# Filler matmuls without a bank dependency, row-form scores and a gate in four pieces, in a planned attention and convolution kernel

## The chip, the core and the metric

The kernel runs on one core of a Trainium2 chip. The core has five engines with queues of their own: TensorE (PE, with its weight loads as PEld), VectorE (DVE), ScalarE (ACT), GpSimd (POOL) and SyncE (SP). The metric is the device time of one execution in microseconds (us).

## The reference

The reference mixes two branches by a gate: `g * a + (1 - g) * b`, where `x` has 2048 rows of 448 values.

```python
g = sigmoid((x * gate_w).sum(-1, keepdims=True))
q = (x @ wq) as 16 heads of 28;  k = x @ wk;  v = x @ wv      # one k and v for all heads
p = softmax(einsum("bhqd,bkd->bhqk", q, k) * 28 ** -0.5)
a = einsum("bhqk,bkd->bhqd", p, v) @ wo
K = einsum("dn,dnl,dn->dl", C, exp(dt * A * l), dt * B).real   # 448 filters, 2048 long
b = causal convolution of x with K, per column, + x * Dskip
```

## The kernel before, in words

**Attention.** The scores are cut into 1024 tiles of 128 keys by 512 queries. Tile t belongs to group t // 64 (one quarter of the queries and four heads), to key block t % 64 // 4, and to head t % 4. The tiles are worked on in 410 *sets* of three and two in turn. Set s has one score step (`qk`), which writes PSUM banks of psS (five are in use in turn), and one exp on ScalarE (L1412), which reads these banks and writes the ring expT, 15 tiles long. A *value step* (`pv`, L1433) multiplies four tiles of the ring by the values and adds them up in bank 6 (psB). After 16 of them VectorE copies the bank (L1157) and normalizes it (L1169). Exps and sets are counted from 0 here.

A score step has two forms. In *row form* (L1357) each tile uses 29 rows of the array, those of its head, so that tiles of different heads run beside each other. In *full form* (L1380) each tile uses all 128 rows with a masked copy of the queries (qM), and the tiles run one behind the other. The last 24 tiles cover 256 queries by two key blocks each (L1368, L1427).

**Convolution.** VectorE builds tables for 14 chunks of 32 columns (L957 to L1008); TensorE multiplies them (the *table product*, L1031, 64 matmuls a chunk) in two halves; VectorE copies each half (L1043), and GpSimd's queue writes it to DRAM (KP). SyncE's queue loads it back as shifted bands T (the *T load*, four DMAs, 56 loads). TensorE convolves (L1098, 128 matmuls for each of 28 convolutions), VectorE scales the result (L1108), TensorE turns it (L1119), and VectorE adds it to O (L1128). Output products of the first three query quarters (L1137) are folded in by L1148. The last quarter ends the kernel: early halves (L1242, added by L1248), the reciprocal of the sums (L1202, L1209, L1228), the product with it (L1232), the last products (L1270, L1276), the adds (L1290, L1293) and the stores.

**What sets the order.** A planner (`schedule`, L188) takes every operation with an estimated duration, its dependencies and a priority (`pr`, smaller goes first). It places them one by one on the engine queues; the engines then work in that order. Dependencies come from the keys that an operation reads and writes (L133 to L155). On TensorE the planner puts in *general fillers* (L1339, matmuls that add zeros) where it expects a pause and little work before it. Beside them there are *warm fillers* (L1333, also adding zeros to bank 6), one for each of 43 early sets (L1398 to L1400). A warm filler writes key `("b", 6)`, so it depends on the value step before it and every later value step depends on it. `opened` (L279) tells whether an accumulation in bank 6 is under way.

**The gate.** Its sigmoid is spread over partitions by matmuls in `prep_gate`: one (L749) is held back until set 30, and four (L760) are one operation, held back until set 35 (`GATE`, L1396). VectorE copies the result (L766), which the convolution needs in L1108.

Of the kernel before, what the change touches and what calls it, by code (L numbers as in the profile page):

```python
# [12 lines left out]
P = 128  # L13
# [35 lines left out]
ROWS = 400  # L49
NEWQ = 15  # L50
# [45 lines left out]
class Prog:  # L96
# [15 lines left out]
    LAZY = {1.15: 200.0, 1.55: 200.0, 1.58: 200.0, 1.6: 200.0}  # L112
    LATE = 1000.0
    FILL, FWIN, FLOW = 215.0, 4000.0, 0.8

    def __init__(self, nc, es):
        self.nc, self.es = nc, es
# [70 lines left out]
    def schedule(self):  # L188
        ops = self.ops
# [11 lines left out]
        ready = {e: [] for e in ENG}  # L201
        rt = [0.0] * n
# [12 lines left out]
        opened = False  # L215
# [8 lines left out]
        while done < n:  # L224
            best = None
            for e in ENG:
                T = free[e]
                for i in ready[e]:
                    o = ops[i]
                    r = max(rt[i], T)  # L230
                    if o.lock is not None:
                        L = min((x for x in locks if x[0] is None), key=lambda x: x[1], default=None)
                        if L is None:
                            continue
                        r = max(r, L[1] + (300.0 if o.pr >= 2 else 0.0))
                    for k in o.comm or ():
                        if k in comm:
                            r = max(r, ops[comm[k]].end)
                    if e == "pe":
                        j = (npe + o.ni - self.FIRST - 1) // self.BLOCK + 1  # L240
                        if j < len(block):
                            r = max(r, block[j])
                            if o.pr >= 1 and block[-1] > r:
                                left = self.FIRST + (len(block) - 2) * self.BLOCK - npe - o.ni
                                r = max(r, block[-1] - left / self.NEED)
                    if o.slot is not None and o.slot[0] == "T" and self.spaced[0] < r < self.spaced[1]:
                        r = max(r, lastT + self.GAP)
                    key = (r, o.pr, i)
                    if best is None or key < best[0]:
                        best = (key, e, i)  # L250
# [25 lines left out]
                mode = o.mode  # L276
            if e == "pe":
                past.append((r, r + o.ns * o.act))
                opened = o.psb == 1 if o.psb else opened  # L279
            if e == "pool" and o.slot is None:  # L280
                for d in reversed(order[e]):
                    if ops[d].slot is None:
# [148 lines left out]
class Kernel:  # L431
# [311 lines left out]
    def prep_gate(self):  # L743
        pg = self.pg
        X = ("gx",)
        px = self.grp()
        ogT = Sub(self.acc, 512)
        self.gate = []
        o = pg.op("pe", lambda e: e.matmul(px.v(0, 16, 0, [[1, 128]]), self.gt.v(0, P, 16, [[1, 16]]),  # L749
                                       self.identg.v(0, P, 0, [[1, P]]), start=True, stop=True, tile_position=(0, 0),  # L750
                                       skip_group_check=True), 400,
              rd=["og", ("kst", 0)], wr=[X], pr=2, lock=px)
        self.gate.append(o.i)
        pg.op("dve", lambda e: e.tensor_copy(ogT.v(0, 16, 0, [[1, 128]]), px.v(0, 16, 0, [[1, 128]])), 200,
              rd=[X], wr=[("acc", 1)], pr=2)

        def mm(e):
            for mu in range(2):
                for par in range(2):
                    r = e.matmul(px.v(0, P, 64 * mu, [[1, 64]]), self.sel.v(0, 16, 128 * (1 + (1 - mu) - par), [[1, P]]),  # L760
                                 ogT.v(0, 16, 64 * par, [[1, 64]]), start=(par == 0), stop=(par == 1), tile_position=(0, 0),
                                 skip_group_check=True)
            return r
        o = pg.op("pe", mm, 800, rd=[("acc", 1)] + [("sel", k) for k in range(3)], wr=[X, "onw"], pr=2)
        self.gate.append(o.i)
        pg.op("dve", lambda e: e.tensor_copy(self.omq.v(0, P, 0, [[1, 128]]), px.v(0, P, 0, [[1, 128]])), 200,  # L766
              rd=[X], wr=["omq"], pr=2, unlock=px)
# [543 lines left out]
    def main(self):  # L1311
# [32 lines left out]
        def qk(s):  # L1344
            ts = sets[s]
            bs = [bank[t] for t in ts]
            bk = [("b", b) for b in bs]

            def row(e):
                if ts[0] >= NLAST:  # L1350
                    for x in range(2):
                        for t, b in zip(ts, bs):
                            r = part(e, t, b, x, True)
                    return r
                for t, b in zip(ts, bs):
                    i, kt, h = dec(t)
                    r = e.matmul(self.psS.v(0, P, 512 * b, [[1, 512]]),  # L1357
                                 kT.v(32 * h, DH + 1, 128 * kt, [[1, 128]]),
                                 qT.v(32 * h, DH + 1, 512 * (i % 2), [[1, 512]]),
                                 start=True, stop=True, tile_position=(32 * h, 0), skip_group_check=True)  # L1360
                return r

            def part(e, t, b, x, row):
                half, kt, h = declast(t)
                kt += x
                o = self.psS.v(0, P, 512 * b + 256 * x, [[1, 256]])
                if row:
                    return e.matmul(o, kT.v(32 * h, DH + 1, 128 * kt, [[1, 128]]),  # L1368
                                    qT.v(32 * h, DH + 1, 512 + 256 * half, [[1, 256]]),
                                    start=True, stop=True, tile_position=(32 * h, 0), skip_group_check=True)  # L1370
                return e.matmul(o, kT.v(0, P, 128 * kt, [[1, 128]]),
                                self.qM.v(0, P, XQ + 512 * h + 256 * half, [[1, 256]]),
                                start=True, stop=True, tile_position=(0, 0), skip_group_check=True)

            def full(e, t, b):
                if t >= NLAST:
                    part(e, t, b, 0, False)
                    return part(e, t, b, 1, False)
                i, kt, h = dec(t)
                return e.matmul(self.psS.v(0, P, 512 * b, [[1, 512]]), kT.v(0, P, 128 * kt, [[1, 128]]),  # L1380
                                self.qM.v(0, P, (i % 2) * XQ + 512 * h, [[1, 512]]),
                                start=True, stop=True, tile_position=(0, 0), skip_group_check=True)
            if s < 6 or s >= 14 and (len(ts) == 3 or ts[0] % 64 < NEWQ or s >= ROWS):
                rd = set()
                for t in ts:
                    i, kt, h = dec(t)
                    rd |= {("q", i % 2), ("kT", (kt if t < NLAST else declast(t)[1]) // 4)}
                o = pg.op("pe", row, 220, rd=sorted(rd, key=str), wr=bk, pr=0, mode="q", ni=2 * len(ts))
                o.act = 0.25 * len(ts)
            else:  # L1390
                for t, b in zip(ts, bs):
                    i, kt, h = dec(t)
                    kt = kt if t < NLAST else declast(t)[1]
                    o = pg.op("pe", lambda e, t=t, b=b: full(e, t, b), 220, rd=[("qM", i % 2), ("kT", kt // 4)],
                              wr=[("b", b)], pr=0, mode="f", ni=2)
            if s in GATE:  # L1396
                pg.after[self.gate[GATE.index(s)]] = o.i
            if s < WARM and ts[0] % 64 < 52 and (ts[0] < 64 or ts[0] % 64 > 14):  # L1398
                f = pg.op("pe", warm, 215, rd=[("cst", 1), "id"], wr=[("b", 6)], pr=1.95)
                pg.after[f.i] = o.i  # L1400
            if s == len(sets) - 2:
                pg.after[o.i] = self.prevset
            self.prevset = o.i
            if s in STORES:
                self.hold.append(o.i)
            es = [ring[t] for t in ts]
            ew = [("e", x) for x in es]
            for t in ts:
                x = ring[t] if t <= RING else 0
                ew += ["Wk"] if x == RING - 1 else ["Wv", "Wvg", "Wm"] if x == RING - 2 else self.xk(2) if 9 <= x < 13 else self.xk(3) if 5 <= x < 9 else []  # L1410
            n = len(ts)
            o = pg.op("act", lambda e: e.activation(expT.v(0, P, 512 * es[0], spread(es, n)),  # L1412
                                                self.psS.v(0, P, 512 * bs[0], spread(bs, n)),
                                                AF.Exp, scale=SQ), 46 + 428 * n, rd=bk, wr=ew, pr=0)
            self.lastexp = o.i
# [118 lines left out]
```

## Time and profile before

| what | value |
|---|---|
| three runs, median | 501.88, 501.09, 500.85; 501.09 us |
| profiled execution | 500.49 us, span 498.7 us |
| mean granted TensorE clock | 0.999 |
| busy: PE, DVE, ACT, POOL | 478.2, 456.0, 484.6, 197.5 us |
| exps (L1412), 410 | 464.8 us busy, 3.5 us idle before them |
| scores, row form (L1357), 684 | 95.7 us busy |
| scores, full form (L1380), 316 | 95.1 us busy |
| general fillers (L1339), 154 | 49.4 us busy (47.2 on psB, 2.2 on psS) |
| warm fillers (L1333), 43 | 16.1 us busy |

A profiled line of a group gives line, engine, operation, the tile written and the tiles read, shapes, count, then busy time, mean ns of one, and the idle time before them with the instruction that ended it. A line of a timeline gives start in us, duration in us, engine, line, operation and count; in brackets stands an idle time and what ended it. Matmuls of a group overlap, so a busy TensorE is not one at its peak: a matmul of 512 columns takes 0.38 us from start to end, and the next may start 0.22 us behind it. Times from one exp to the next are taken from the start times in the trace.

### The profile page before, as it was taken

What the parts mean: (1) busy time and instruction counts of PE and PEld (TensorE: products, weight loads), DVE (VectorE), ACT (ScalarE), POOL (GpSimd) and SP (SyncE); (2) the same over time, 40 slices, a digit from 0 to 9 for tenths busy, and PEclk for the clock granted to TensorE, in tenths of its full rate; (3) what the DMA queues carried; (4) which work ended last, traced back from release to release, by engine and by line L of the source; (5) the groups of instructions that cost most, each with busy time, mean ns of one, the idle gap of its engine ahead of it and who ended that gap; (6) DMA issues with size and microseconds to landing.
All of it is one profiled execution on the core that took longest, in us unless ns stands there. A gap on an engine that the chain in (4) does not pass through costs nothing.

```text
span 498.7 us, 17357 instructions
## 1 busy us (share of the span) xinstructions
PE 478.2 (96%) x7643; PEld 217.7 (44%) x7643; DVE 456.0 (91%) x868; ACT 484.6 (97%) x436; POOL 197.5 (40%) x362
## 2 busy tenths in 40 slices
PE   8899999999999999999999999999999999999997
PEld 6432242453434435453452543545334354445543
DVE  6999999999999999999999999989999999992225
ACT  6999989999999999999999999999999999999995
POOL 8411034342242466276265456552733342521110
PEclk9999999999999999999999999999999999999999
DMA  8945008719248783945729595594690849657842
GB/s 252 268 57 113 1 16 229 213 34 315 77 118 265 204 217 87 308 108 165 242 36 268 155 288 138 141 220 112 171 265 19 231 129 340 213 164 215 257 131 70
DMA packets 91767, 85.44 MB, mean 171 GB/s; under 512 B 24970, under 2 KB 86716, under 8 KB 91692
## 3 DMA queue, kind: packets, MB, share of 16 engines
q1 hardware_dynamic: 80794, 72.49, 49.8%
q0 software_dynamic: 10624, 11.70, 10.5%
q8 instruction: 60, 0.98, 0.8%
q10 hardware_dynamic: 274, 0.14, 0.1%
q14 instruction: 15, 0.12, 0.1%
HBM read 76.36 MB, written 5.23 MB: 164 GB/s over the span
## 4 chain that ended last, share of the span: by engine, by line
ACT 77%; PE 15%; DMA 2%; SPq 0%; issue 0%
ACT expT L1412 77%; PE psS L1380 2%; PE psS L1357 2%; PE psB L1433 2%; DMA T<-KP_scratch 2%; PE psX L1098 1%; PE psS L1098 1%; PE psS L1031 1%; PE psB L1333 1%; PE psS L1368 1%; PE psS L1242 0%; PE psB L1427 0%; SPq L166 0%; PE psX L1031 0%; PE psX L1119 0%; PE psB L1339 0%
## 5 line engine op out<-in xcount | busy, mean ns | idle before, releaser
L1412 ACT ACTIVATE expT<-psS 128x1536 bf16<-128x1536 f32 (+1 forms) x410 | 464.8, 1363 | 3.5 <-PE psS L1357 1.4
L972 DVE TENSOR_TENSOR tab<-tab,mbf 128x512 bf16<-128x512 bf16 (+4 forms) x140 | 139.2, 996 | 0.0
L1357 PE MATMUL psS<-qT,kT 29*128 29x512 bf16 x684 | 95.7, 385 | 10.5 <-ACT expT L1412 6.4
L1433 PE MATMUL psB<-expT,vaug 128*32 128x512 bf16 x1000 | 99.7, 390 | 0.2 <-DVE acc L1157 0.2
L1380 PE MATMUL psS<-qM,kT 128*128 128x512 bf16 x316 | 95.1, 383 | 0.8
L166 POOL DMA_DIRECT2D KP_scratch<-kstg x104 | 58.1, 565 | 75.5 <-DVE kstg L1043 74.0
L987 DVE TENSOR_TENSOR tab<-tab 128x256 bf16<-128x256 bf16 (+4 forms) x140 | 77.0, 571 | 0.0
L1433 PEld LDWEIGHTS psB<-expT,vaug 128*32 128x32 bf16 x1000 | 25.6, 93 | 72.9 <-issue 69.9
L1357 PEld LDWEIGHTS psS<-qT,kT 29*128 29x128 bf16 x684 | 23.7, 91 | 62.9 <-ACT expT L1412 51.9
L166 POOL DMA_DIRECT2D U<-in_A_x_dram x60 | 39.9, 669 | 25.0 <-DMA U<-in_A_x_dram 10.3
L166 POOL DMA_DIRECT2D qM<-qT x64 | 32.5, 516 | 39.4 <-DVE qT L889 29.3
L1339 PE MATMUL psB<-ident,one 128*128 128x512 bf16 x146 | 47.2, 384 | 0.0
L1098 PEld LDWEIGHTS psS<-T,U 128*26 128x26 bf16 (+3 forms) x1792 | 35.7, 138 | 14.9 <-issue 10.2
L166 POOL DMA_DIRECT2D rdenB<-R_scratch x60 | 31.0, 523 | 28.0 <-DMA R_scratch<-denT 27.9
L1098 PE MATMUL psS<-T,U 128*26 128x128 bf16 (+3 forms) x1792 | 41.0, 226 | 1.1 <-DMA T<-KP_scratch 1.1
L1098 PE MATMUL psX<-T,U 128*26 128x128 bf16 (+3 forms) x1600 | 38.9, 227 | 0.7 <-issue 0.7
L1098 PEld LDWEIGHTS psX<-T,U 128*26 128x26 bf16 (+3 forms) x1600 | 32.6, 139 | 11.9 <-issue 9.5
L166 POOL DMA_DIRECT2D denT<-acc x15 | 10.8, 717 | 56.4 <-DVE acc L1157 47.7
L1001 DVE TENSOR_TENSOR tab<-tab,tmp 128x1984 bf16<-128x1984 bf16 x28 | 32.5, 1177 | 0.0
L1380 PEld LDWEIGHTS psS<-qM,kT 128*128 128x128 bf16 x316 | 19.5, 97 | 24.8 <-ACT expT L1412 15.3
L995 DVE TENSOR_TENSOR tmp<-tmp,mq 128x64 bf16<-128x64 bf16 (+4 forms) x70 | 25.3, 361 | 0.3
L918 DVE TENSOR_TENSOR msq<-T 128x512 f32<-128x512 f32 (+1 forms) x40 | 24.6, 616 | 0.0
(191 smaller groups left out, 511.9 us busy)
## 6 DMA issues: line engine op xcount, KB each, us to landing
T<-KP_scratch SPq DMA_DIRECT2D x212, 272.0 KB, 5.6
rdenB<-R_scratch POOLq DMA_DIRECT2D x60, 64.0 KB, 2.5
U<-KP_scratch SPq DMA_DIRECT2D x12, 272.0 KB, 4.9
U<-in_A_x_dram SPq DMA_DIRECT2D x20, 112.0 KB, 4.6
qM<-qT POOLq DMA_DIRECT2D x64, 32.0 KB, 3.9
tab<-in_A_x_dram SPq DMA_DIRECT2D x4, 448.0 KB, 5.2
KP_scratch<-kstg POOLq DMA_DIRECT2D x104, 16.0 KB, 1.7
xT<-XS_scratch POOLq DMA_DIRECT2D x3, 448.0 KB, 4.3
```

The source lines that it names most:

```text
L166: return [e.dma_start(o, i, **kw) for o, i in pairs]
L918: pg.op("dve", lambda e: e.tensor_tensor(m2(msq), z2, z2, ALU.mult), el(2 * n), rd=[kr, ki] + first, wr=["msq"], pr=pr)
L972: mul = lambda e, o, a, b: e.tensor_tensor(o, a, b, ALU.mult)
L987: vo(lambda e, dv=dv, tv=tv, k=k: e.tensor_tensor(dv, dv, tv, ALU.add if k else ALU.subtract), n, [kt[k], kd[k]], [kd[k]], 1.92 if lv else ...
L995: vo(lambda e, w=w, lv=lv: e.tensor_tensor(rho.v(0, P, (32 - 2 * w) * 2, [[64, 32], [2, w], [1, 2]]), rho.v(0, P, (32 - w) * 2, [[64, 32], ...
L1001: vo(lambda e, k=k: e.tensor_tensor(tab.v(0, P, FM + k * FP + 2, [[64, 32], [2, 31], [1, 2]]), tab.v(0, P, lm + k * PL + 62, [[64, 32], [- ...
L1098: r = e.matmul(ps.v(32 * j, 32 - m0, 128 * k, [[1, 128]]), self.U.v(0, P, (4 * gi + j) % UA // UC * UW + (2 * m0 + par) * UC + (4 * gi + j ...
L1339: return e.matmul(t.v(0, P, off, [[1, 512]]), self.one.v(0, P, 2, [[0, P]]), self.ident.v(0, P, 0, [[0, 4], [1, P]]), start=b != 6, stop=b ...
L1357: r = e.matmul(self.psS.v(0, P, 512 * b, [[1, 512]]), kT.v(32 * h, DH + 1, 128 * kt, [[1, 128]]), qT.v(32 * h, DH + 1, 512 * (i % 2), [[1, ...
L1380: return e.matmul(self.psS.v(0, P, 512 * b, [[1, 512]]), kT.v(0, P, 128 * kt, [[1, 128]]), self.qM.v(0, P, (i % 2) * XQ + 512 * h, [[1, 51 ...
L1412: o = pg.op("act", lambda e: e.activation(expT.v(0, P, 512 * es[0], spread(es, n)), self.psS.v(0, P, 512 * bs[0], spread(bs, n)), AF.Exp, ...
L1433: r = e.matmul(self.psB.v(32 * h, 32, 0, [[1, 512]]), vaug.v(0, P, 32 * kt, [[1, 32]]), expT.v(0, P, 512 * ring[t], [[1, 512]]), start=(kt ...
```

## The change

There are three edits, and a rule in the planner that goes with the first.

- A warm filler no longer names bank 6 as written, so it neither waits for value steps nor holds them back. Instead it is marked `psb = 3`. The planner places such an operation only while `opened` holds. If an operation of priority 0 or less becomes ready while the filler would run (up to 40 ns before its end), the filler's start is put behind it. A filler leaves `opened` as it is.
- A set of three tiles is always in row form; before, sets 6, 8, 10 and 12 were in full form.
- The gate's four matmuls are four operations, of which only the first is held back until set 35.

```diff
+    NEAR = 40.0
...
+                    if o.psb == 3:
+                        if not opened:
+                            continue
+                        for x in ready["pe"]:
+                            if ops[x].pr <= 0.0 and r < rt[x] < r + o.ns - self.NEAR:
+                                r = max(rt[x], T) + ops[x].ns
...
-                opened = o.psb == 1 if o.psb else opened
+                opened = o.psb == 1 if o.psb in (1, 2) else opened
...
-        def mm(e):
-            for mu in range(2):
-                for par in range(2):
-                    r = e.matmul(px.v(0, P, 64 * mu, [[1, 64]]), self.sel.v(0, 16, 128 * (1 + (1 - mu) - par), [[1, P]]),
-                                 ogT.v(0, 16, 64 * par, [[1, 64]]), start=(par == 0), stop=(par == 1), tile_position=(0, 0),
-                                 skip_group_check=True)
-            return r
-        o = pg.op("pe", mm, 800, rd=[("acc", 1)] + [("sel", k) for k in range(3)], wr=[X, "onw"], pr=2)
+        for mu in range(2):
+            for par in range(2):
+                o = pg.op("pe", lambda e, mu=mu, par=par: e.matmul(
+                    px.v(0, P, 64 * mu, [[1, 64]]), self.sel.v(0, 16, 128 * (1 + (1 - mu) - par), [[1, P]]),
+                    ogT.v(0, 16, 64 * par, [[1, 64]]), start=(par == 0), stop=(par == 1), tile_position=(0, 0),
+                    skip_group_check=True), 200, rd=[("acc", 1)] + [("sel", k) for k in range(3)], wr=[X, "onw"], pr=2)
+                if mu + par == 0:
+                    o1 = o
+        o = o1
         self.gate.append(o.i)
...
-            if s < 6 or s >= 14 and (len(ts) == 3 or ts[0] % 64 < NEWQ or s >= ROWS):
+            if s < 6 or len(ts) == 3 or s >= 14 and (ts[0] % 64 < NEWQ or s >= ROWS):
...
-                f = pg.op("pe", warm, 215, rd=[("cst", 1), "id"], wr=[("b", 6)], pr=1.95)
+                f = pg.op("pe", warm, 215, rd=[("cst", 1), "id"], pr=1.95)
+                f.psb = 3
```

Since the planner works through all operations anew, the order of TensorE, VectorE, GpSimd and SyncE changes over the whole kernel.

## Prediction

> **What bounds the kernel now.** I read the page first: the chain that ended last, then the groups.
>
> ```profile
> ACT 77%; PE 15%; DMA 2%; SPq 0%; issue 0%
> ...
> L1412 ACT ACTIVATE expT<-psS 128x1536 bf16<-128x1536 f32 (+1 forms) x410 | 464.8, 1363 | 3.5 <-PE psS L1357 1.4
> ```
>
> The chain is ScalarE's 410 exps, one behind the other; 15% of it is TensorE, where an exp waited. So the question is how often the exps wait. I took their start times from the trace. From one exp to the next it is 1.331 us after three tiles and 0.904 us after two (medians). 205 of the one and 204 of the other make 457.3 us, but the first exp starts at 21.71 and the last at 491.82, 470.1 us later. 2.6 of the 12.8 us between are other ScalarE work behind the first exp. So 10.2 us are lost, and a change of TensorE's order can win no more than that ahead of the last exp. The larger losses: 0.65 us together ahead of exps 6, 8, 10, 12 (0.13, 0.27, 0.13, 0.11); 0.53 ahead of exp 36; 1.27 ahead of exp 42; 1.08 ahead of exp 266; 1.83 in six pieces from 460 to 479 us. The other 4.8 us are small pieces.
>
> The timelines of ScalarE, then of TensorE, show three of these places:
>
> ```profile
> 34.01 31.97 ACT L1412 ACTIVATE expT<-psS 128x1536 bf16<-128x1536 f32 x28 [0.16 <-PE psS L1380]
> 66.20 6.88 ACT L1412 ACTIVATE expT<-psS 128x1536 bf16<-128x1536 f32 x6 [0.23 <-PE psS L1357]
> 74.19 5.97 ACT L1412 ACTIVATE expT<-psS 128x1536 bf16<-128x1536 f32 x5 [1.11 <-PE psB L1433]
> ```
>
> ```profile
> 64.85 0.77 PE L760 MATMUL psS<-acc,onT 16*128 16x64 f32 x5
> 65.35 0.39 PE L1357 MATMUL psS<-qT,kT 29*128 29x512 bf16 x2
> 65.46 0.49 PE L760 MATMUL psS<-acc,onT 16*128 16x64 f32 x3
> 65.79 0.38 PE L1357 MATMUL psS<-qT,kT 29*128 29x512 bf16 x1
> ...
> 72.78 0.60 PE L1333 MATMUL psB<-ident,cst 128*128 128x512 bf16 x2
> 73.22 0.59 PE L1380 MATMUL psS<-qM,kT 128*128 128x512 bf16 x2
> 73.74 0.40 PE L1433 MATMUL psB<-expT,vaug 128*32 128x512 bf16 x4
> 74.08 0.39 PE L1333 MATMUL psB<-ident,cst 128*128 128x512 bf16 x1
> 74.40 0.40 PE L1433 MATMUL psB<-expT,vaug 128*32 128x512 bf16 x4
> ...
> 327.50 0.40 PE L1098 MATMUL psS<-T,U 128*32 128x128 bf16 x12 [1.12 <-DMA T<-KP_scratch]
> ```
>
> At 64.85 the gate's matmuls (one operation, eight records) stand ahead of a score set. At 72.78 value matmuls (L1433) come late, two warm fillers (L1333) among them: none ran between 68.36 and 73.74, and the exp waits for a place in the ring of 15 tiles. At 327.50 a convolution waits for its T load, and the scores behind it with it.
>
> **The change, part by part.** The built order of the changed kernel has the same counts but for: 12 more scores in 29-row form and 12 fewer in full form, 6 fewer general fillers (L1339: 151 for 154 with all banks); warm fillers stay at 43. Everything else is a new order, chosen by the planner. Each part is compared set by set.
>
> *Rows (sets 6, 8, 10, 12).* Three full-form scores take 0.81 us (33.16, L1380 x3), three in row form 0.39 (L1357 x3). That is 0.42 per set, more than any of the four losses. TensorE pays three warm fillers behind set 7 (0.22 each), but sets 6 and 7 with these come to about 2.65 us and the pairs beside them to 2.1, against 2.235 of exps. I take -0.55; ends -0.65 and 0.
>
> *Gate.* The four matmuls now stand two behind set 35, one behind 36, one behind 37. Ahead of set 36 there is half of the 0.9 us, but a value step and a filler stand there too. I take -0.35; ends -0.53 and +0.2.
>
> *Fillers without the bank.* Before, each warm filler wrote bank 6, so every later value step depended on it. In the new order, sets 38 to 46 have a value step at nearly every place that is due, between pieces of the table product (L1031), and the three in a row are gone. The ring is then never full. I take -1.2 of the 1.27; ends -1.27 and -0.6. What is late next: set 40 and set 42 behind 16 table matmuls (0.6), some 0.1 us, within that.
>
> *The T wait at 327.* A side effect. This load was issued at 317.12, behind convolution matmuls of set 257, and landed at 327.46. In the new order those stay in set 257, but the first use moves from behind set 265 to behind set 266, 1.13 us later, with a filler ahead of it: just the wait. I take -1.0; ends -1.08 and 0.
>
> *The stretch from 460 to 479.* Here TensorE has as much work as ScalarE. With durations from this stretch (40 conv matmuls 0.74, a value step 0.3, a row set 0.32), sets 380 to 399 hold 22.9 us of it before and 22.0 after, against 22.4 of exps. One 0.69 us wait at 469.0 has no releaser ("issue"), and T loads land one behind the other there; both can come again. I take -0.5; ends -1.5 and +0.8.
>
> *New waits for T loads.* I compared, load by load, landing and first use. The table products come 2 sets later nearly everywhere (0 to 4), the convolutions 0 to 15 sets later, 6 earlier in one place. Two loads lose cover: the 38th had 1.54 us and is used 1 set closer to its issue; the 41st had 2.06 us, its table product is one set later and its use one set earlier, which leaves about -0.2. I take +0.5 for these and other unplanned waits; ends 0 and +1.5.
>
> *DVE as cover.* VectorE idles under 4 us from 20 to 449, and its last table ends at 448.6; the table products started 0.2 to 4.3 us behind their tables. If ScalarE runs 3 us ahead, this would be late next. But those products are 2 sets (2.24 us) later in the order, and VectorE's own 1.16 us wait at 330 goes with the T wait. So I charge nothing; without that cover it would cost up to 1 us.
>
> *The tail.* Behind the last exp (end 492.41) the order is longer. Before:
>
> ```profile
> 493.69 0.21 DVE L1228 RECIPROCAL T<-psS 128x8 f32<-128x8 f32 x1
> 493.90 0.62 DVE L1290 TENSOR_TENSOR O<-O,psS 128x448 bf16<-128x448 bf16 x1
> 494.70 0.42 DVE L1232 TENSOR_TENSOR onT<-acc,psS 128x256 bf16<-128x256 f32 x1 [0.18 <-PE psS L1217]
> 495.58 0.62 DVE L1290 TENSOR_TENSOR O<-O,psS 128x448 bf16<-128x448 bf16 x1 [0.46 <-PE psS L1270]
> ```
>
> One add of 0.62 stands between the reciprocal and the product that the last outputs need (L1232). In the new order two stand there (L1248 and L1290), since the last convolution's transposes (16 of L1119, 0.45 us) and the early outputs of tile 15 moved behind the last exp. Two adds from a reciprocal that ends near 494.16 end at 495.3, so L1232 starts at about 495.24, +0.54. Behind it stand four output matmuls, not two: 0.93 us for 0.55, +0.38. Together +0.9; ends +0.5 and +1.5. The store of columns 320 on (issued 490.05, last packet 492.9) comes after the last exp too, but its packets would end about 4.3 us behind that exp, ahead of the last tiles' packets.
>
> **Sum.** -0.55 -0.35 -1.2 -1.0 -0.5 +0.5 +0.9 = -2.2 us. The profiled execution took 500.49 us (498.7 of span and 1.8 around it), 0.6 under the median of the three runs shown, 501.09. So 498.3 profiled, and 498.9 as a median. This measurement can tell about 0.2% from no change, 1.0 us.
>
> **Rivals.**
>
> *Taken back (0.16).* The transfers and the "issue" waits are drawn anew with any order, and as many come as went: the T wait and the late stretch are then of no worth, new waits 1.0. That gives -0.55 -0.35 -1.2 +1.0 +0.9 = -0.2, 500.9. For it: 4.8 us of small losses that I can't place. Against: only two waits near 1 us in the whole trace came from a load or from "issue".
>
> *More (0.15).* The late stretch keeps pace (-1.5), nothing new waits, tail +0.7: -3.9, 497.2. For it: 22.0 us of work in 22.4.
>
> *Clock (0.06), the slower side.* Ahead of the first value step four warm fillers go (24.21 to 27.04), since the bank isn't open yet. From 24.0 to 27.4 TensorE was busy for 82% of the time; four times 0.22 us less leave 57%. If the granted clock halves for 3.4 us there, half of that work, 1.7 us, comes late, and ScalarE waits for it. One such stretch gives 500.6; two give -2.2 + 3.4, 502.3, and that is slower than before. It decides from 1.3 stretches on. Against it stands the emptiest stretch before, here with the columns TensorE busy, weights, VectorE, ScalarE, GpSimd, granted clock, DMA share, GB/s:
>
> ```profile
> 12.00:14.00 2.00, 0.87 (x12) 0.56 (x10) 2.00 (x3) 1.90 (x2) 1.79 (x4) 1.00 1.06 250
> ```
>
> TensorE is busy for 0.87 of 2 us, and the clock stays at 1.00. The Trainium skill ("TensorE: Matmul & The Clock Gate", section "A second HAM failure mode: psum-queue depth-cycling") says that cycling through PSUM banks with 512-column matmuls leaves short pauses in which the clock falls and rises again. By that rule this kernel would show it before the change already; the trace disagrees, its mean granted clock is 0.999.
>
> *It doesn't do what it says (0.01):* the built order shows that it does.
>
> The forecast itself has 0.62 (497.9 to 499.9). Faster by over 0.2%, under 500.1: 0.62 + 0.15, and 0.03 of the first rival, 0.80. Within 0.2%: 0.13. Slower: 0.07, the clock and the worst of what is taken back. The range leaves about a tenth out on either side: 497.2 to 501.0.
>
> **What would show it.** Right: exps 6 to 12 at 0.904 us behind the one before; no exp behind L1433 near 73; under 0.3 us lost at exp 36; no wait at exp 266, but perhaps at exp 327; L1232 some 2.8 us behind the last exp's end (2.29 before) and the last L1293 some 4.3 (3.36). Wrong: a granted clock under 1.00 between 20 and 40 us; L1031 waiting for DVE tab in the sum; more than 1 us lost at new places between 80 and 450 us.

## The result and the profile after

The changed kernel took 497.74 us (median of 5, 497.46 to 498.08), the kernel before on the same chip 501.01 (median of 5, 500.31 to 501.88): ratio 0.9934, 95% interval [0.992, 0.9949]. On a second chip it took 496.88 beside 500.78, ratio 0.9913 [0.9894, 0.9931]. So it gained 3.3 and 3.9 us where 2.2 were forecast. Its first profiled execution took 498.08 us with a span of 496.3, clock 0.999; the one of before took 500.49 and 498.7.

The page of after, the chain by engine and the group of the exps:

```profile
ACT 86%; PE 8%; issue 0%
...
L1421 ACT ACTIVATE expT<-psS 128x1536 bf16<-128x1536 f32 (+1 forms) x410 | 464.1, 1347 | 1.0 <-PE psS L1388 0.6
```

TensorE's share of the chain is 8% for 15%, and the exps (now L1421; lines from the gate on are 8 or 9 higher) waited 1.0 us for 3.5. The timeline of ScalarE from 28 to 80 us, where before had three waits, is one row without a bracket:

```profile
27.60 53.14 ACT L1421 ACTIVATE expT<-psS 128x1024 bf16<-128x1024 f32 x47
```

The timeline of TensorE shows why. The gate's matmuls, two records each, no longer stand ahead of the score set of exp 36 as one block: two run beside it. From 69 us on a value step (L1442) stands between the pieces of the table product (L1039), with no filler among them; and at 324.85 a convolution finds its T load there:

```profile
63.90 0.32 PE L766 MATMUL psS<-acc,onT 16*128 16x64 f32 x1
64.06 0.38 PE L1365 MATMUL psS<-qT,kT 29*128 29x512 bf16 x1
...
69.16 0.40 PE L1442 MATMUL psB<-expT,vaug 128*32 128x512 bf16 x4
69.49 0.42 PE L1039 MATMUL psX<-tab 128*64 128x128 bf16 x8
69.84 0.60 PE L1388 MATMUL psS<-qM,kT 128*128 128x512 bf16 x2
70.38 0.40 PE L1442 MATMUL psB<-expT,vaug 128*32 128x512 bf16 x4
...
324.85 0.47 PE L1106 MATMUL psX<-T,U 128*32 128x128 bf16 x16
```

The timeline of VectorE behind the last exp, which ended at 488.69:

```profile
490.05 0.21 DVE L1236 RECIPROCAL T<-psS 128x8 f32<-128x8 f32 x1 [0.20 <-PE psS L1210]
490.26 0.62 DVE L1256 TENSOR_TENSOR O<-O,psS 128x448 bf16<-128x448 bf16 x1
490.80 0.61 DVE L1298 TENSOR_TENSOR O<-O,psX 128x448 bf16<-128x448 bf16 x1
491.44 0.42 DVE L1240 TENSOR_TENSOR onT<-acc,psS 128x256 bf16<-128x256 f32 x1
```

Two adds stand between the reciprocal and the product, as forecast. The product starts 2.75 us behind the last exp's end (2.29 before), the last copy (L1301, 492.88) 4.19 (3.36), and the span ends 7.6 behind it (6.34).

The two spans differ by 2.4 us: the exps lose 3.3 less, the tail takes 1.3 more, and the first exp starts 0.44 earlier (21.27 for 21.71). Over all profiles below the first exp starts at 21.27 to 22.28, whatever the kernel, so that part is not the change's.

### The profile page after: what moved, and what is told of

Same layout as the page of the kernel before. It is cut to its first block, busy times and chain, and to the rows that moved or that the text cites. A ratio compares the mean times of both kernels' runs of the same rounds, so it can differ in the third digit from the quotient of the medians.

```text
span 496.3 us, 17350 instructions
## 1 busy us (share of the span) xinstructions
PE 476.6 (96%) x7640; PEld 217.8 (44%) x7640; DVE 455.5 (92%) x868; ACT 483.8 (97%) x436; POOL 196.2 (40%) x362
## 4 chain that ended last, share of the span: by engine, by line
ACT 86%; PE 8%; issue 0%
ACT expT L1421 86%; PE psX L1106 1%; PE psS L1388 1%; PE psB L1442 1%; PE psS L1365 1%; PE psS L1376 1%; PE psS L1106 0%; PE psS L1250 0%; PE psB L1436 0%; PE psS L1278 0%; PE psX L1127 0%; PE psS L1145 0%; PE psB L1347 0%; PE psS L1225 0%; PE psS L1210 0%
## 5 line engine op out<-in xcount | busy, mean ns | idle before, releaser
L1421 ACT ACTIVATE expT<-psS 128x1536 bf16<-128x1536 f32 (+1 forms) x410 | 464.1, 1347 | 1.0 <-PE psS L1388 0.6
L1365 PE MATMUL psS<-qT,kT 29*128 29x512 bf16 x696 | 97.4, 384 | 9.2 <-ACT expT L1421 4.8
L1442 PE MATMUL psB<-expT,vaug 128*32 128x512 bf16 x1000 | 100.3, 390 | 0.5 <-issue 0.5
L1388 PE MATMUL psS<-qM,kT 128*128 128x512 bf16 x304 | 92.0, 384 | 1.4 <-issue 0.7
L1442 PEld LDWEIGHTS psB<-expT,vaug 128*32 128x32 bf16 x1000 | 25.6, 93 | 71.7 <-issue 69.6
L1106 PE MATMUL psX<-T,U 128*26 128x128 bf16 (+3 forms) x1792 | 44.2, 226 | 0.2 <-DVE O L1136 0.2
L1106 PEld LDWEIGHTS psX<-T,U 128*26 128x26 bf16 (+3 forms) x1792 | 37.2, 138 | 14.6 <-issue 10.0
L1106 PE MATMUL psS<-T,U 128*26 128x128 bf16 (+3 forms) x1600 | 37.7, 226 | 0.0
L1106 PEld LDWEIGHTS psS<-T,U 128*26 128x26 bf16 (+3 forms) x1600 | 32.4, 138 | 11.4 <-issue 8.0
L1388 PEld LDWEIGHTS psS<-qM,kT 128*128 128x128 bf16 x304 | 18.5, 97 | 23.5 <-ACT expT L1421 14.5
```

The lines of the kernel that those rows point to most:

```text
L1106: r = e.matmul(ps.v(32 * j, 32 - m0, 128 * k, [[1, 128]]), self.U.v(0, P, (4 * gi + j) % UA // UC * UW + (2 * m0 + par) * UC + (4 * gi + j ...
L1365: r = e.matmul(self.psS.v(0, P, 512 * b, [[1, 512]]), kT.v(32 * h, DH + 1, 128 * kt, [[1, 128]]), qT.v(32 * h, DH + 1, 512 * (i % 2), [[1, ...
L1442: r = e.matmul(self.psB.v(32 * h, 32, 0, [[1, 512]]), vaug.v(0, P, 32 * kt, [[1, 32]]), expT.v(0, P, 512 * ring[t], [[1, 512]]), start=(kt ...
```

## The experiments

Each profile was read in one way: the time from one exp to the next over 1.331 or 0.904 us, summed by stretches of exps. "Under 1" counts the executions with a mean granted clock of 0.997 or less. The ratio is to before on the same chip. "Listed" kernels keep an order that is written out.

| kernel | median, before | ratio, 95% | under 1 | exps 1-13 | 14-34 | 35-50 | 51-260 | 261-280 | 281-380 | 381-409 | sum | behind |
|---|---|---|---|---|---|---|---|---|---|---|---|---|
| before, first profile | 501.01 | | | 1.0 | 0.1 | 1.8 | 2.6 | 1.2 | 1.3 | 2.1 | 10.2 | 6.3 |
| p_rows (listed) | 500.40, 500.65 | 0.9995 [0.9979, 1.0011] | 6 of 12 | 0.3 | 0.5 | 1.9 | 3.8 | 0.3 | 1.4 | 2.4 | 10.6 | 6.3 |
| p_ring (listed) | 500.26, 500.65 | 0.9997 [0.9977, 1.0017] | 6 of 12 | 1.0 | 0.1 | 1.3 | 2.8 | 0.7 | 1.2 | 1.7 | 8.8 | 6.4 |
| p_load (listed) | 500.30, 500.65 | 0.9994 [0.9982, 1.0005] | 4 of 11 | 1.1 | 0.1 | 1.8 | 2.6 | 0.6 | 1.3 | 2.4 | 9.9 | 6.3 |
| p_all (listed) | 500.26, 500.65 | 0.9986 [0.9972, 1.0001] | 5 of 12 | 0.3 | 0.5 | 1.5 | 2.8 | 0.6 | 1.3 | 1.2 | 8.3 | 6.4 |
| p_clk (listed) | 499.42, 500.22 | 0.9979 [0.9965, 0.9993] | 0 of 12 | 1.0 | 0.1 | 1.8 | 2.7 | 0.7 | 1.2 | 2.7 | 10.3 | 6.4 |
| rows | 500.16, 500.78 | 0.9984 [0.9967, 1.0001] | 1 of 12 | 0.3 | 0.2 | 2.0 | 3.0 | 0.6 | 1.3 | 1.6 | 9.0 | 6.9 |
| fill | 501.72, 500.78 | 1.0014 [0.9999, 1.0029] | 11 of 12 | 1.1 | 0.1 | 0.7 | 3.7 | 1.8 | 1.7 | 1.6 | 10.6 | 6.7 |
| no_gate | 500.35, 500.22 | 0.9988 [0.9969, 1.0008] | 6 of 12 | 0.3 | 0.2 | 0.7 | 3.5 | 0.6 | 1.9 | 1.9 | 9.1 | 7.5 |
| no_fill | 499.06, 500.22 | 0.9976 [0.9956, 0.9995] | 6 of 12 | 0.3 | 0.2 | 1.9 | 3.4 | 2.0 | 1.4 | 1.1 | 10.2 | 6.4 |
| after, first profile | 497.74, 501.01 | 0.9934 [0.9920, 0.9949] | 1 of 5 | 0.3 | 0.2 | 0.2 | 3.0 | 0.2 | 2.6 | 0.4 | 6.9 | 7.6 |
| after_2 | 496.88, 500.78 | 0.9913 [0.9894, 0.9931] | 0 of 6 | 0.3 | 0.2 | 0.2 | 3.0 | 0.2 | 1.1 | 1.2 | 6.3 | 7.4 |
| tail (listed) | 497.22, 500.78 | 0.9941 [0.9912, 0.9969] | 4 of 12 | 1.3 | 0.2 | 0.2 | 3.0 | 0.2 | 1.1 | 0.5 | 6.6 | 7.3 |
| tail_f (listed) | 497.40, 500.22 | 0.9945 [0.9924, 0.9965] | 2 of 7 | 0.3 | 0.2 | 0.2 | 3.0 | 0.2 | 1.1 | 0.6 | 5.7 | 7.5 |

The stretches and the time from the end of the last exp to the end of the span (last column) are those of one profile of each kernel, and some losses come and go between executions of one order. Four of these profiles (p_rows, fill, no_fill, tail) hold one fall of the clock each between the first exp and the last. Of the executions of before, 49 of 94 had a clock of 0.997 or less, and took 501.05 for 499.90 (medians).

### One wait at a time, in the old order

The theory after the result: each edit takes its wait away for good. The rival: the luck of a new order, or a later wait that takes it back. So the order of before was written out for all engines, and the planner takes the next operation of the list:

```diff
+            tok = seq.pop(0)
...
                 for i in ready[e]:
+                    if tok >= 0 and i != tok:
+                        continue
                     o = ops[i]
```

**p_rows**: the 29-row edit, its operations in the old places.

```diff
-            if s < 6 or s >= 14 and (len(ts) == 3 or ts[0] % 64 < NEWQ or s >= ROWS):
+            if s < 6 or len(ts) == 3 or s >= 14 and (ts[0] % 64 < NEWQ or s >= ROWS):
```

> The order of before is written out on every engine and kept; only the three score matmuls of sets 6, 8, 10 and 12 become 29-row ones. Theory (each wait that is removed stays removed): exps 6, 8, 10, 12 start 0.90 to 0.91 us behind the one before, 0.65 us less is lost there, the last exp starts 0.6 us earlier and the kernel takes 500.4 for 501.0. Rival 1 (taken back): the exps are ahead by 0.65 at exp 12, but a later wait for a load, a table or a value step gives it back, so the last exp starts as before and the time is 501.0. Rival 2 (the gain of the whole change is the luck of a new order): makes no difference to this kernel, whose order is the old one; then the parts held in the old order must together fall well short of 3 us.

**p_ring**: TensorE's order from set 40 on (s score set, k eight table matmuls, v value step, f warm filler; the text on record counts these sets one too low). The warm fillers of sets 36 to 49 name no bank:

```diff
-s40 k k s41 k k k s42 f f s43 v f v f f v s44 f v
+s40 v k k s41 v k k k s42 f f s43 v f f f s44 v f
```

> The order of before but for four value steps, which stand one to three sets earlier (behind sets 39, 40, 42 and 43), ahead of the warm fillers that held them back; the warm fillers of sets 36 to 49 do not name bank 6, the others do. Theory: the loss ahead of exp 42 falls from 1.27 to under 0.3 us and stays away; 499.8 for 501.0. Rival 1 (taken back): the loss at exp 42 goes, but the table products behind it, or a later wait, take it back within some sets, and the time is 500.8 to 501.0.

**p_load**: 44 convolution matmuls (c, four each) behind set 267.

```diff
-c c c s266 c c c c c c c c s267 v c
+s266 s267 v c c c c c c c c c c c c
```

> The order of before but for the first 11 operations (44 matmuls) of the convolution that waited for its T load at 327: they stand behind set 267 and its value step, two sets later. Theory: no wait at exp 266, the load has landed by the first use; 1.0 us less, 500.0 for 501.0. Rival 1 (taken back): TensorE has no room for the 0.8 us that it skipped, or the next T load, whose buffer comes free later, is waited for: the loss moves to exps 268 to 290 and the time is 500.7 to 501.0.

**p_all**: the three together, and the gate in four operations.

> The three edits of the other kernels of this call in one, and the gate's four matmuls apart (two behind set 35, one behind 36, one behind 37), else the order of before. Theory: 0.65 + 1.27 + 1.08 + 0.35 = 3.3 us less ahead of the last exp and the tail of before kept: 497.7 for 501.0, as much as the changed kernel gained with a longer tail. Rival 1: the later waits take back half or more, over 499.4. Rival 2 (luck of the new order, mainly the stretch from 460 to 479): this kernel still loses its 1.8 us there, and ends at or above 499.

Measured: at its own place each edit did at least part of what it should, but for p_load. Exps 1 to 13 lose 0.3 for 1.0 in p_rows and p_all. Exps 35 to 50 lose 0.5 less in p_ring; 0.58 stays at exp 42, because in the old order three pieces of the table product stand behind the value step that now comes in time:

```profile
71.42 0.61 PE L1470 MATMUL psS<-qM,kT 128*128 128x512 bf16 x2
71.96 0.40 PE L1523 MATMUL psB<-expT,vaug 128*32 128x512 bf16 x4
72.29 0.89 PE L1121 MATMUL psS<-tab 128*64 128x128 bf16 x24
73.12 0.39 PE L1447 MATMUL psS<-qT,kT 29*128 29x512 bf16 x3
```

But the times hardly fell: 0.4 us or less by the medians, and p_all, forecast at 497.7, took 500.26. Both theories lose something. Part is taken back: with 0.7 won at exps 1 to 13, exps 14 to 34 lose 0.4 more, as a value step then waits 0.6 us for VectorE to copy bank 6 (0.60 in p_rows, 0.58 in p_all). And the T wait at 327 had been one execution's: p_rows, p_ring and p_clk keep that part of the old order, and in their profiles no convolution waits there (exps 261 to 280 lose 0.3 to 0.7, not 1.2). Two of them wait for another load instead, at 338, for 0.35 (p_ring) and 0.30 us (p_clk). p_load took away what is mostly not there.

### The edits alone, planned anew

**after_2** is the changed kernel once more. **fill** and **rows** are before with one edit each, the first and the second of the change's diff.

> The changed kernel once more, beside kernels with one edit, since the times of the kernel before spread from 499.1 to 503.2 us on the last chip. If the first measurement holds, 3.3 us under the kernel before of this call (ratio 0.993) and the exps lose some 7 us as in its first profile (first exp to last exp start 466.8 us). If the gain was half the luck of that chip or of its profile, the ratio is 0.996 or more.

> The kernel before with the filler edit alone (no bank in the keys, and the planner's rule), planned anew: table products 0.9 sets later on the mean, 2.1 in the changed kernel. Theory A (the direct waits): exp 42 loses nothing, 0.6 to 1.3 us less; the small waits of exps 6 to 12 and 36 stay; 499.9 for 501.0. Theory B (the new order itself, by later table products and convolutions, is what gains): more than its own wait, 2 us or more less, 499.0 or under.

> The kernel before with the row-form edit alone, planned anew. Theory A: the 0.65 us of exps 6 to 12 go, exps 36 and 42 stay, 0.4 less by the median (what the same edit gave in the old order at full clock), 500.6 for 501.0. Theory B: any new order can gain or lose 1 to 2 us; then it lies more than 1 us away from that, on either side.

The gain of the whole change held, with 3.9 us. The edits alone gave none of it that the intervals tell from nothing: rows 0.6 us less, fill 0.9 us more. In fill the ring wait is gone (exps 35 to 50 lose 0.7, which is the gate), so the edit does its work; but its profile loses 1.0 more than the first of before from 51 to 260 and 0.6 more from 261 to 280, and 11 of 12 executions had a lower clock. The trace places most of that. Of the first, 0.76 is exp 238, where the clock stands at one half from 292.2 on (the two rows below, with the columns TensorE busy, weights, VectorE, ScalarE, GpSimd, granted clock, DMA share, GB/s); of the second, 0.74 is exp 271, behind a wait of TensorE of 1.09 us that nothing in the profile released ("issue").

```profile
288.70:291.70 3.00, 2.01 (x21) 0.55 (x20) 3.00 (x5) 3.00 (x4) 0.75 (x2) 1.00 0.88 231
292.20:295.60 3.40, 3.40 (x31) 1.16 (x27) 3.40 (x4) 2.73 (x3) 0.79 (x2) 0.50 0.97 263
```

**no_gate** and **no_fill** are the changed kernel with one edit undone (no_fill also without the planner's rule that goes with it):

```diff
-        for mu in range(2):
-            for par in range(2):
-                o = pg.op("pe", lambda e, mu=mu, par=par: e.matmul(
+        o = pg.op("pe", mm, 800, rd=[("acc", 1)] + [("sel", k) for k in range(3)], wr=[X, "onw"], pr=2)
```

```diff
-                f = pg.op("pe", warm, 215, rd=[("cst", 1), "id"], pr=1.95)
-                f.psb = 3
+                f = pg.op("pe", warm, 215, rd=[("cst", 1), "id"], wr=[("b", 6)], pr=1.95)
```

> The changed kernel with the gate's matmuls as one operation again, planned anew. Theory A (the edits' own waits): 0.35 us more than the changed kernel, some 3 us under before. Theory B (most of the gain beside 0.7 at exps 1 to 13 and 1.6 at exps 35 to 50 is the draw of a new order: load and instruction waits, late stretch, clock dips): more than 1 us from the changed kernel, most likely slower.

> The changed kernel without the filler edit (29-row sets and the gate in four), planned anew. Theory A: the ring wait of 1.3 us at exp 42 is back, exps 1 to 13 and 36 are as in the changed kernel, 1.0 to 1.2 us under before. Theory B: more than 1 us away from that; by the rows alone (0.16% under before) and the filler edit alone (0.14% over it) anything from 499 to 501.5 where before takes 500.8.

For the whole time this speaks for the order. Without the gate's split, worth 0.4 us at its place, the kernel takes 500.35, as much as before: exps 51 to 260 lose 0.6 more, 281 to 409 1.4 more than in after_2, and half of the executions have a lower clock. In its profile 2.8 us of the loss stand at exps 200, 377 and 397, each behind an "issue" wait (0.92, 0.52 and 1.49 us). Without the filler edit the median is 499.06, which the direct sum had right. Its profiled execution took 500.21; the ring wait is back in it (1.78 at exp 42), and it lost 1.76 at exp 264 for a T load and 0.68 at exp 82, where the clock had fallen at 116.6. Two of these waits in the timelines of TensorE:

```profile
325.75 0.40 PE L1099 MATMUL psS<-T,U 128*32 128x128 bf16 x12 [1.74 <-DMA T<-KP_scratch]
```

```profile
475.31 0.64 PE L1105 MATMUL psS<-T,U 128*32 128x128 bf16 x28 [1.49 <-issue]
```

Such pieces hide what the edits do. Leave out of each sum the pieces of 0.4 us or more that stand behind a T load, a fall of the clock or an "issue" wait: six profiles of the old order keep 7.9 to 8.5 us, rows 8.2, fill 8.1, no_fill 7.8, no_gate 6.3, and four of the changed order (after, after_2, tail, tail_f) 5.6 to 5.8. What is left in no_gate and no_fill is 0.7 and 2.1 more than in the changed order, not far from their own waits (0.4 and 1.7), as theory A has it; the whole time goes with theory B, since a new order also draws these pieces anew. This rests on one profile of each kernel, and rows and fill alone stay in or near the range of the old order.

### The clock

Where the clock fell, the windows show it. The columns are as above. First p_rows, then the kernel called tail below:

```profile
173.00:176.00 3.00, 1.90 (x16) 0.49 (x16) 3.00 (x5) 3.00 (x4) 1.36 (x3) 1.00 0.88 269
176.30:179.70 3.40, 3.40 (x29) 1.11 (x27) 3.08 (x4) 2.35 (x3) 2.23 (x5) 0.51 0.92 293
```

```profile
24.30:27.30 3.00, 1.74 (x24) 0.98 (x21) 3.00 (x8) 3.00 (x5) 0.79 (x1) 1.00 0.93 201
27.60:31.00 3.40, 3.40 (x17) 0.72 (x16) 3.40 (x5) 2.52 (x3) 0.00 (x0) 0.54 0.42 16
```

In both, TensorE was busy for some 0.6 of 3 us, then the clock was one half for 3.4 us, and an exp came late: exp 134 of p_rows by 1.2 us (the text on record below calls it 133), exp 4 of tail by 1.0. The two other falls followed pauses that were less empty: 2.01 of 3 us in fill, and 2.17 of 3 us from 113.3 in no_fill. Other executions pass the same pause at full clock: in the profile of after_2, TensorE is busy for 1.74 of the 3 us from 23.8 and the clock stays at 1.00. The Trainium skill ("TensorE: Matmul & The Clock Gate", section "Part 1: The HAM clock gate (the "warmup" mystery)") says that the gate watches activity in a free-running window of about 3.4 us. That agrees with the 3.4 us measured, and a window that does not start with the kernel would explain why the same order loses the clock in some executions only; no run here shows the window itself.

**p_clk**: the order of before with three fillers in the pause at 173 and one in that at 116.

```diff
-s131 v s132 v s133
+s131 v f f s132 v f s133
```

> The order of before with four more general fillers, three where TensorE was busy for only 0.64 of 3 us (from 172.7, sets 131 and 132) and one at 116 (0.70). In an execution of the same order with 29-row sets the granted clock fell to half from 176.3 on, and 1.2 us were lost at exp 133; of the executions of before, 18 in 35 on one chip and 23 in 29 on the other had a mean granted clock under 1.000, and took 1.3 us longer than the others by the median. Theory (these dips come from the pause at 173, in executions where the clock's window falls on it): nearly all executions at 1.000, and the median falls by 0.7 to 1.2 us, to that of the executions of before at full clock. Rival (the dips fall anywhere or come with the chip): as many dips as in before, no gain.

It held: none of 12 executions under 1, 499.42 for 500.22, with the same losses ahead of the exps as before. Since both pauses were filled, the run does not tell them apart. The places fit in the other kernels too: rows, with TensorE busy for 2.86 of the 3 us from 172.7, had 1 of 12; fill, with pauses at 24, 289 and 330, had 11 of 12.

**tail** and **tail_f** test the longer tail and the pause at 24; tail_f has both of the edits below, tail the first.

```diff
-        for tt in range(4):
+        for tt in range(3):
             self.early(tt)
...
-                for g in range(2, 3):
+                for g in range(2 if tt < 3 else 0, 3):
```

> The changed kernel, its order kept up to the last exp. Behind it the early output of tile 15 is no operation of its own: its two matmuls go into the accumulation of the last output, so that VectorE has one add of 0.62 less between the last reciprocal and the product, and the last value matmul stands directly behind the reciprocal on TensorE. Theory (the longer tail is these adds and matmuls): the product starts 2.3 us behind the last exp's end for 2.75, the last copy 3.4 to 3.6 for 4.19, and the kernel takes 0.6 to 0.8 us less than the changed kernel. Rival (the stores of the early columns end last, whatever the order behind the exps): the copy is earlier but the span ends 7.6 us behind the last exp as before, no gain.

```diff
-                f = pg.op("pe", warm, 215, rd=[("cst", 1), "id"], pr=1.95)
+                f = pg.op("pe", warm, 215, rd=[("cst", 1), "id"], wr=[("b", 6)] if s < 4 else [], pr=1.95)
```

> The kernel with the shortened tail, and four warm fillers put back where they stood before the change, ahead of the first value step (24 to 27 us); they name bank 6 again. The changed kernel leaves TensorE busy for only 0.58 of the 3 us from 23.8 there; in one profile of it the clock fell to half from 27.7 on, and 5 of 12 executions were under 1.000. Theory: no execution or one under 1.000, and a median of 496.6 on the chip on which the changed kernel took 496.9. Rival (fillers there delay the first scores): exps 1 to 6 lose 0.3 us more and the median is not under that of the changed kernel.

The tail's theory fell. The product does start 2.37 us behind the last exp (tail_f), but TensorE then has nine output matmuls in a row, and the last copy comes 4.13 behind the exp for 4.19. VectorE's add was only one of two chains of the same length. The rival on record, the stores, was not put to the test, since the copy moved by 0.06 us only: in all four profiles of the changed order the first of five stores lands 5.6 to 5.9 us behind the last exp, and the last 1.3 us behind the first, so an earlier copy alone may not end the kernel sooner. What gain there is (executions at 0.999 or more: 496.69 for after_2's 496.88) is within the spread. In tail_f, exps 1 to 13 lose 0.3, so the fillers at 24 delay nothing there; 2 of 7 executions were under 1, against none of 6 and 1 of 5 of the changed kernel and 4 of 12 of tail. That is too few to say that they help. No kernel here is shown to beat the changed one.

## Why the prediction was right, and where it was not

The forecast's side and its range held (498.9, 497.2 to 501.0); its sum was 1.2 us short, 0.2 outside the likeliest case's own range (497.9 to 499.9). By its steps:

- **Rows, gate, fillers: right, a little small.** Exps 1 to 13 lose 0.72 less (forecast 0.55), exps 35 to 50 lose 1.6 less (0.35 + 1.2). Why the value steps were late is now clear from the order: each depended on the warm filler ahead of it, the filler's priority (1.95) is behind that of the table products (1.15), and so the value step (0.5) waited for table products that it should have passed. fill removes this wait, and p_ring more than half of it (0.58 of 1.27 stays). The count of general fillers on record mixes two counts; in the traces they are 140 for 146 on psB and 150 for 154 in all. Nothing rests on it.
- **The T wait at 327: mis-sized.** Forecast -1.0. It stood in the one profile there was; three other profiles of that part of the order do not have it. The stretch around it loses 0.3 to 0.7 in these and 0.2 in the new order: -0.4 at most.
- **The stretch from 460 to 479: mis-sized the other way.** Forecast -0.5. Exps 381 to 409 lose 1.2 to 2.7 in six profiles of the old order (mean 2.1) and 0.4 to 1.2 in four of the new (mean 0.7): -1.4. Of that, 0.8 are exps behind "issue" waits (391 and 396 in the old order, 1.0 in the mean of six; 398 in one of four of the new, 0.2), which the forecast let come again. Without them the stretch gains 0.6, near the forecast; the forecast's count, 22.0 us of work for 22.9 against 22.4, points that way, but no run tests it.
- **New waits: right in size, wrong in kind.** No T load was waited for. The first profile of after has two "issue" waits, 0.66 and 0.46 us, and exps 281 to 380 lose 1.5 more there than in after_2, tail and tail_f, which have neither; after_2 has one of 0.42 at 473.7. Exps 14 to 34 and 51 to 260 lose 0.5 more than before.
- **VectorE as cover: right.** No matmul of a table product has idle time that VectorE ended; their weight loads wait 0.4 us for it at most.
- **The tail: mis-sized.** Forecast +0.9, measured +1.3 and +1.1. The product (+0.46, forecast 0.54) and the last copy (+0.83, forecast 0.92) came nearly as worked out. The rest is the stores. That of the early columns was said to end ahead of the last tiles': it took 4.7 us to land, not 3.2, with the others issued meanwhile, and the last tile's store 2.4 for 1.9.
- **The clock: the step that failed.** It was argued from a mean of 0.999 in one profile, as a risk of the change alone, at 24 to 27 us. The pause there is real (TensorE busy for 58%, as worked out) and did halve the clock in tail's profile, at 1.0 us for the exps where 1.7 was priced. But the larger effect has the other sign: before loses its clock in half of its executions, most likely at the pause near 173, which the new order does not have. By medians that is 1.2 us on the second chip (500.78 for 499.56 at 0.999 or more), 0.6 and 0.3 on the two others.

Together, -0.7 - 1.6 - 0.4 - 1.4 + 0.5 for the small losses, +0.4 for "issue" waits (1.5 in one of four profiles) and +1.2 for the tail are -2.0; executions at 0.999 or more differ by 2.7 (499.56 to 496.88), and the clock adds 1.2. So 0.7 us is not placed by stretches; the start of the first exp, which differs by up to 1.0 between executions, is as large.

The rival "taken back" was right for single edits and wrong for the whole. Only exps 1 to 50 belong to the edits: they lose 2.2 us less in the changed kernel and 1.8 less in no_gate; whether the end of the kernel sees them was decided by the rest of the order, which each edit drew anew. What makes the changed kernel's order better in its late stretch and less exposed to "issue" waits and falls of the clock was not isolated, so this part of the gain may be luck of the order.

## What to carry to other kernels

When a planner makes the order, an edit's local gain and its total are two things: write the old order out and measure the edit in it, then count the new order as a draw, with several executions of it. One profile shows one execution: a wait for a load or for instructions that stands in it may be absent from the next, so take it at its mean over profiles, and look for such pieces before an order is called better or worse. Before a filler is taken away, look at TensorE's busy share over 3 us, not at the mean clock.

## What the runs showed of the hardware that was not expected

- The granted clock falls to half for 3.4 us behind a pause in which TensorE is busy for 0.58 to 0.72 of 3 us (four profiles), in some executions of the same program and not in others. Executions of before with a lower clock took 1.2 us longer by the medians. Four fillers of 0.22 us removed it (0 of 12 for 14 of 30).
- TensorE waits with no releaser, of 0.42 to 1.49 us, appear up to three times in an execution, at other places in the next one; in the trace of before such a wait (0.69 us at 469.0) follows a fetch on the instruction queue that landed at 468.27. Each of the 17 such waits of 0.4 us or more in the 14 profiles ended 1.2 to 1.6 us behind the landing of a 16 KB packet on instruction queue q8, which has 60 such packets an execution. So they are most likely waits for instructions; no run changed the fetches. The Trainium skill ("Runtime: NRT & Kernel Launch", section "Instruction fetch mechanics") says that crossing from one 16 KiB block of instructions to the next is mostly hidden; the trace agrees for most crossings, and these waits are larger than that.
- Stores that are under way together land later. In before the store of 384 KB landed 3.2 us after its issue, ahead of the next issue, and the last one of 112 KB took 1.9; in after four more were issued before the first landed, which took 4.7, and the others landed 0.3 us apart, the last one 2.4 us after its issue.
